# Zero matmuls in TensorE's waits ahead of the first MoE matmul, batch 0's scores by head pairs, and new figures in the planner of the order

## The chip, the core and the metric

The kernel runs on one core of one Trainium2 chip. The metric is the device time of one execution in microseconds. TensorE multiplies matrices, ScalarE computes exp and tanh and copies results out, VectorE transposes 32x32 blocks and does the elementwise work, GpSimd issues the loads, SyncE the stores.

## The reference

```python
# q, k, v: (8 batches, 12 heads, 448 tokens, 64), float32
scores = matmul(q, k.T) / sqrt(64)
attn = exp(scores - max(scores))
attn = attn / (sum(attn) + 1e-9)
x = matmul(attn, v)                       # heads side by side: 3584 tokens x 768
h = x @ w_in                              # 768 x 2048
g = h * sigmoid(h)
out = g @ w_out                           # 2048 x 768, float32
```

## The kernel before

Loads convert float32 to float16 on the way. The 12 heads of a batch are handled four at a time (a head group, `hg`); the four heads occupy the four groups of 32 rows of the 128 partitions. A **unit** is a batch, a head group and a range of queries. In batch 0 the queries are split in two halves of 224, so that units 0, 1, 2 are the first half of the three head groups and units 3, 4, 5 the second; from unit 6 (batch 1) on a unit has all 448 queries.

The stages of a unit are:

* K and Q are loaded (`load_k` L214, `load_q` L219) and transposed on VectorE (`turn_k` L257, `turn_q` L279); V is loaded (`load_v` L230).
* **Scores** (`scores` L307, matmul at L295): keys come in four chunks `c` of up to 128. Results go to PSUM tiles `s`, of which there are two (`s_ring`); one holds two heads (a head pair `y`, 0 or 1) times 448 columns. In batch 0 a tile holds two chunks of 224 queries.
* **exp** (`expo` L327, ScalarE at L331): one 128x896 activation for each `s` tile, four in a batch 0 unit, into a tile `E` (11 of them, `e_ring`).
* **Attend** (`attend` L355, matmul at L347), in three parts: part 0 multiplies E by ones and gives the sums, parts 1 and 2 multiply by V. The results sit in PSUM tiles tagged `m`, of which there are four (`m_ring`). `inverse` (L378, three VectorE steps) turns the sums into 1/sum, `norm` (L394) scales parts 1 and 2 into `xT`.
* **MoE**: `ffn1` (L411) makes six matmuls for one 128-wide slice f of the 2048 hidden columns, `tanh` (L423, ScalarE) and `gate` (L428, VectorE) follow; `ffn2` (L441) makes 16 matmuls for 128 tokens and half of the 768 columns, `store` (L454) copies and stores. Their results share the four `m` tiles with attend.

**The order is made by a planner** that runs in Python when the program is built. `Order` (L69) keeps a modelled time `now` and, for each engine, when it is free. It picks the next piece of work for TensorE at each moment it is free: scores when they are ready and due (`PACE`), else attend, else the first MoE job whose inputs are there. For ScalarE and VectorE it picks, among the operations that are ready, the one with the lowest ready time plus bias. Loads go out in a fixed list on GpSimd's queue (L518 to L540): K and Q of batch 0's three head groups, V of batch 0, Q of its second half, 12 loads of w_in (f 0 to 7), K and Q of batch 1's first group, 12 loads of w_in (f 8 to 15), and so on with w_out in two halves. `Order.step` (L108) says when a load is thought to have landed, from `DMA_RATE` and `DMA_LAT`. What the planner settles is the order of instructions on each engine, nothing else: on the chip every instruction still waits for its own inputs, and instructions of one engine run in that order.

Before all of it, 13 matmuls of zeros (`NWARM`, L856) stand at the head of TensorE's program. The first MoE matmul needs `xT` of units 0, 1 and 2 and the first 12 loads of w_in.

Of the kernel before, what the change touches and what calls it, by code (L numbers as in the profile page):

```python
# [10 lines left out]
FP32 = mybir.dt.float32  # L11
# [5 lines left out]
SWITCH = 0.094  # L17
PE_OUT = 0.20
HOP = 0.10
DMA_RATE = 0.36  # L20
DMA_LAT = 2.0


def mm(n):
    return n / 2400.0 + 0.0026


def act(n):
    return n * 0.000833 + 0.093
# [39 lines left out]
class Order:  # L69


    def __init__(self):
        self.now = 0.0
        self.free = {e: 0.0 for e in ("PE", "ACT", "DVE", "POOL")}
        self.wait = {"ACT": [], "DVE": []}
        self.pool = []
        self.dma_free = 0.0
        self.out = []
        self.mode = None
        self.busy = {e: 0.0 for e in self.free}  # L80
# [27 lines left out]
    def step(self):  # L108

        soon = []  # L110
        for eng in ("ACT", "DVE"):
            if self.free[eng] > self.now:
                soon.append(self.free[eng])
                continue
            best = None
            for op in self.wait[eng]:
                at = op.ready()
                if at is None:
                    continue
                if at > self.now:  # L120
                    soon.append(at)
                elif best is None or at + op.bias < best[0]:
                    best = (at + op.bias, op)
            if best:
                self.wait[eng].remove(best[1])
                self.start(best[1])
                soon.append(self.free[eng])
        if self.free["POOL"] > self.now:
            soon.append(self.free["POOL"])
        elif self.pool:  # L130
            op, mb, ring, gate = self.pool[0]
            at = 0.0
            if ring is not None:
                at = ring.when(1)
            if at is not None and gate is not None:
                g = gate()
                at = None if g is None else max(at, g)
            if at is not None and at <= self.now:
                self.pool.pop(0)
                if ring is not None:  # L140
                    ring.take()
                self.start(op)
                self.dma_free = max(self.dma_free, self.now + 1.0) + mb / DMA_RATE
                op.done = self.dma_free + DMA_LAT - 1.0
                soon.append(self.free["POOL"])
            elif at is not None:
                soon.append(at)
        return soon
# [3 lines left out]
def kernel(  # L152
# [9 lines left out]
    nc = tc.nc  # L162
# [6 lines left out]
    TPP = S // 32  # L169
# [9 lines left out]
    NT = 2 * S // 128  # L179
    OH = DM // 2  # L180
    PACE = 2.6
    NWARM = 13
    LONE = NG + 1
    NE, NGT = 11, 22
    attn_scale = 1.0 / (D**0.5)
# [28 lines left out]
    def load_k(b, hg):  # L214
        t = sb.tile([128, TPP, 2, 32], FP16, name=f"rk_{b}_{hg}", tag="rk", bufs=3)
        nc.gpsimd.dma_start(out=t, in_=group_of(k, b, hg))  # L216
        rawk[(b, hg)] = t

    def load_q(n):  # L219
        b, hg, g0, g1 = units[n]  # L220
        t = sb.tile([128, g1 - g0, 2, 32], FP16, name=f"rq_{n}", tag="rq", bufs=4)
        nc.gpsimd.dma_start(out=t, in_=group_of(q, b, hg)[:, D * g0 : D * g1])  # L222
        rawq[n] = t
# [243 lines left out]
    units = []  # L467
# [12 lines left out]
    MB = 1e-6 * 4 * 32 * HG * D  # L480

    def plan_k(b, hg):
        ld_k[(b, hg)] = od.load(MB * TPP, lambda: load_k(b, hg), rk_ring)

    def plan_q(n):
        ld_q[n] = od.load(MB * (units[n][3] - units[n][2]), lambda: load_q(n), rq_ring)

    def plan_v(b, hg0, hg1):
        made = []
# [87 lines left out]
    def queue_ffn1(b, g0, g1):  # L577
        t0, t1 = 32 * g0, 32 * g1
        for f in range(NFF):

            def run(f=f):
                if b % 2 == 0 and g0 == 0:
                    g_ring.take()
                op = Op("PE", NDC * mm(t1 - t0), lambda: ffn1(b, f, t0, t1), tail=PE_OUT)
                m_ring.take()
                od.on_pe(op, "full")
                th = od.add(
                    Op("ACT", act(t1 - t0), lambda: tanh(b, f, t0, t1), [op], -1, tail=0.2)
                )
                g = Op(  # L590
                    "DVE",
                    (t1 - t0) / 960.0 + 0.13,
                    lambda: gate(b, f, t0, t1),
                    [th],
                    -0.3,
                    then=m_ring.give,
                )
                g_op.setdefault((b, f), []).append(od.add(g))
                ffn1_left[b] -= 1

            ring = g_ring if b % 2 == 0 and g0 == 0 else None
            moe.append(([x_op[(b, cc, g0)] for cc in range(NDC)] + ld_win[f], ring, run))
            ffn1_left[b] += 1

    def queue_ffn2(u, t, half, bs):
        def run():
            op = Op("PE", NFF * mm(OH), lambda: ffn2(u, t, half), tail=PE_OUT)
            m_ring.take()
            od.on_pe(op, "full")
            od.add(  # L610
                Op("ACT", act(OH), lambda: store(u, t, half), [op], -0.3, then=m_ring.give)
            )
            ffn2_left[u] += 1
            if ffn2_left[u] == 2 * NT:
                for _ in range(NFF):
                    g_ring.give(op.done)

        def deps():
            made = list(ld_wout[half])
            for b in bs:  # L620
                for f in range(NFF):
                    if len(g_op.get((b, f), ())) < (2 if b == 0 else 1):
                        return None
                    made += g_op[(b, f)]
            return made

        moe.append((deps, None, run))
# [45 lines left out]
    qk_seq, av_seq = [], []  # L673
    for ns in jobs:
        if len(ns) == 1:
            split = ((0,), (1,)) if ns[0] < 3 else ((0, 1),)
            qk_seq += [(ns, c, ys) for c in range(NCH // per_burst(ns[0])) for ys in split]
        else:
            qk_seq += [([n], c, (0, 1)) for n in ns for c in range(NCH - 1)]
            qk_seq.append((ns, 3, (0, 1)))  # L680
        av_seq += [(ns, part) for part in range(3)]
# [58 lines left out]
    def av_at():  # L740
        if not av_seq:
            return None
        ns, part = av_seq[0]
        deps = []
        for n in ns:
            if len(exp_op.get(n, ())) < 2 * NCH // per_burst(n):
                return None
            deps += exp_op[n]
            if part:
                deps += ld_v[units[n][:2]] + rdn_op.get(n, [None])  # L750
        at = at_of(deps)
        av_data["at"] = at
        m = m_ring.when(len(ns))
        if at is None or m is None:
            return None
        return max(at, m)
# [28 lines left out]
    def after_av(n, part, op, nq):  # L785
        b, hg, g0, g1 = units[n]
        if part == 0:
            made = []
            for step, busy in enumerate((nq / 960.0 + 0.15, 0.2, nq / 960.0 + 0.15)):
                r = Op(  # L790
                    "DVE",
                    busy,
                    lambda step=step: inverse(n, step),
                    made[-1:] or [op],
                    0.5,
                )
                made.append(od.add(r))
            made[0].then = m_ring.give
            rdn_op[n] = made
        else:  # L800
            x = Op(
                "DVE",
                nq / 960.0 + 0.13,
                lambda: norm(n, part),
                [op] + rdn_op[n],
                -1,
                then=m_ring.give,
            )
            x_op[(b, 2 * hg + part - 1, g0)] = od.add(x)
            if part == 2:  # L810
                after_x(n)

    while True:
        plan_turns(qk_seq[0][0][0] + 4 if qk_seq else NU)
        soon = od.step()
        if od.free["PE"] <= od.now:
# [2 lines left out]
            av_data["at"] = None  # L819
            qk, av = qk_at(), av_at()  # L820
            wait = av_data["at"]
            if wait is not None and wait <= od.now - 6 and not (av is not None and av <= od.now):
                moe_i = None
                soon.append(min([x for x in m_ring.free if x>od.now] or [od.now+0.1]))
            if qk is not None and qk <= od.now and (od.now >= pace["next"] or moe_i is None):
# [21 lines left out]
        later = [x for x in soon if x > od.now]  # L847
        if not later:
            break
        od.now = min(later)  # L850
    assert not (qk_seq or av_seq or moe or any(od.wait.values()) or od.pool)


    z = ps.tile([128, 512], FP32, name="z", tag="m", bufs=4)
    for i in range(NWARM):
        nc.tensor.matmul(out=z, lhsT=zeros[:, 0:128], rhs=zeros, start=True, stop=True)  # L856
    for _, _, fn in sorted(od.out, key=lambda x: x[:2]):
        fn()

# [29 lines left out]
```

The softmax here doesn't subtract the row's maximum and nothing guards it: scores larger than these inputs give would overflow.

## Time and profile before

| | us |
|---|---|
| median of the 4 runs | 426.08 |
| lowest and highest | 425.25, 426.41 |
| the profiled execution, its own time | 426.1 |
| its span (first to last instruction) | 424.3 |
| TensorE busy in the span | 415.1 (98%) |
| ScalarE, VectorE, GpSimd busy | 242.4, 193.6, 95.3 |

In the views, PE is TensorE's matmuls, PEld its weight loads, DVE VectorE, ACT ScalarE, POOL GpSimd, SP SyncE; a q behind a name is an engine's queue of instructions that are not counted as busy. L295 is line 295 of the kernel. The clock that is shown (PEclk) is the one granted to TensorE, as a share of full speed. Matmuls overlap, so that a busy TensorE is not one at its peak.

### The profile page before, as it was taken

To read this page: it belongs to the slowest core of one execution; us is meant where nothing else is said; L and a number is where in the kernel's file an instruction comes from. 1 tells how busy PE (TensorE), PEld (TensorE's weight loads), DVE (VectorE), ACT (ScalarE), POOL (GpSimd) and SP (SyncE) were. 2 spreads that over 40 slices of the span, in tenths; PEclk is the share of its full clock that TensorE was granted. 3 is DMA by queue.
4 is the path that set the end of the run, shared out by engine and by line. 5 is a ranking of instruction groups with operands and counts; after the bars stand their busy time and mean duration, and the time that the engine had idled before them with its cause. 6 is when DMAs were issued, how large, how long until landed. Compare 5 with 4: busy or idle time off the path is not lost.

```text
span 424.3 us, 9512 instructions
## 1 busy us (share of the span) xinstructions
PE 415.1 (98%) x3933; PEld 213.0 (50%) x3933; DVE 193.6 (46%) x404; ACT 242.4 (57%) x373; POOL 95.3 (22%) x175
## 2 busy tenths in 40 slices
PE   7899999999999999999999999999999999999996
PEld 3577765444544444444344545544445555565563
DVE  4568746667433585725577154512354214403400
ACT  3678976697465777667766753465773114414411
POOL 6775556530004407200440700000000000000000
PEclk9579999999999999999999999999999999999999
DMA  8999999790024906712391941012100221031033
GB/s 114 202 195 187 148 189 212 120 173 5 11 66 66 205 3 89 125 44 53 33 163 24 148 99 39 2 28 52 36 2 9 53 62 29 2 74 39 0 75 75
DMA packets 37980, 34.45 MB, mean 81 GB/s; under 512 B 11953, under 2 KB 36401, under 8 KB 37937
## 3 DMA queue, kind: packets, MB, share of 16 engines
q0 software_dynamic: 27184, 22.82, 36.6%
q1 hardware_dynamic: 10656, 10.93, 10.1%
q8 instruction: 31, 0.51, 0.5%
q10 hardware_dynamic: 96, 0.10, 0.1%
q14 instruction: 13, 0.10, 0.1%
HBM read 45.61 MB, written 11.01 MB: 133 GB/s over the span
## 4 chain that ended last, share of the span: by engine, by line
PE 93%; DMA 2%; ACT 1%; POOL 1%; DVE 1%; issue 0%; ACTq 0%; DVEq 0%; POOLq 0%
PE o L445 35%; PE h L414 33%; PE a L347 14%; PE s L295 11%; DMA rk<-in_k_dram 2%; ACT E L331 1%; POOL V L235 1%; DVE KT L271 0%; POOL rq L222 0%; POOL rk L216 0%; DVE QT L282 0%; DVE g L432 0%; ACT ost L457 0%; ACTq L457 0%; DVEq L271 0%
## 5 line engine op out<-in xcount | busy, mean ns | idle before, releaser
L331 ACT ACTIVATE E<-s 128x896 f16<-128x896 f32 (+1 forms) x172 | 149.0, 914 | 24.6 <-PE s L295 23.4
L414 PE MATMUL h<-xT,w_in_t 128*128 128x448 f16 (+1 forms) x864 | 153.6, 332 | 0.8 <-DVE g L432 0.8
L445 PE MATMUL o<-w_out_t,g 128*128 128x384 f16 x896 | 152.5, 327 | 0.0
L432 DVE SCALAR_TENSOR_TENSOR g<-th,h 128x448 f16<-128x448 f16 (+1 forms) x144 | 79.7, 563 | 98.8 <-ACT th L425 96.8
L445 PEld LDWEIGHTS <-g 128*128 128x128 f16 x896 | 84.7, 98 | 65.1 <-issue 11.6
L414 PEld LDWEIGHTS <-w_in_t 128*128 128x128 f16 x864 | 80.7, 98 | 69.5 <-issue 13.8
L425 ACT ACTIVATE th<-h 128x448 f16<-128x448 f32 (+1 forms) x144 | 71.6, 505 | 53.6 <-PE h L414 52.1
L457 ACT COPY ost<-o 128x384 f32<-128x384 f32 x56 | 26.8, 478 | 99.5 <-PE o L445 92.3
L235 POOL DMA_DIRECT2D V<-in_v_dram x88 | 48.8, 569 | 134.8 <-PE a L347 115.4
L295 PE MATMUL s<-QT,KT 32*128 32x448 f16 (+4 forms) x864 | 55.0, 349 | 3.2 <-ACT E L331 2.6
L271 DVE STREAM_TRANSPOSE KT<-rk 128x256 f16<-128x256 f16 (+2 forms) x96 | 31.6, 378 | 44.6 <-PE s L295 26.4
L400 DVE SCALAR_TENSOR_TENSOR xT<-a,rdn 128x448 f16<-128x448 f32 (+1 forms) x54 | 28.9, 567 | 35.1 <-PE a L347 34.8
L347 PE MATMUL a<-E,V 128*32 128x448 f16 (+3 forms) x864 | 42.3, 348 | 0.0
L295 PEld LDWEIGHTS <-KT 32*128 32x128 f16 (+2 forms) x864 | 17.1, 103 | 31.9 <-issue 30.5
L347 PEld LDWEIGHTS <-V 128*32 128x32 f16 (+2 forms) x864 | 19.2, 99 | 23.5 <-issue 16.3
L383 DVE STREAM_TRANSPOSE sT<-a 128x448 f32<-128x448 f32 (+1 forms) x27 | 14.9, 578 | 27.0 <-PE a L347 27.0
L282 DVE STREAM_TRANSPOSE QT<-rq 128x896 f16<-128x896 f16 (+1 forms) x27 | 26.3, 974 | 0.6 <-DMA rq<-in_q_dram 0.5
L347 PE MATMUL a<-E,ones 128*32 128x448 f16 (+4 forms) x432 | 21.8, 349 | 0.0
L222 POOL DMA_DIRECT2D rq<-in_q_dram x27 | 15.4, 572 | 4.6 <-DMA rk<-in_k_dram 1.5
L347 PEld LDWEIGHTS <-ones 128*32 128x32 f16 (+2 forms) x432 | 9.5, 99 | 12.7 <-issue 9.0
L216 POOL DMA_DIRECT2D rk<-in_k_dram x24 | 13.9, 578 | 4.0 <-DMA w_out_t<-in_moe_w_out_dram 1.9
L392 DVE STREAM_TRANSPOSE rdn<-inv 128x448 f32<-128x448 f32 (+1 forms) x27 | 14.5, 562 | 0.1
(12 smaller groups left out, 32.6 us busy)
## 6 DMA issues: line engine op xcount, KB each, us to landing
out_dram<-ost SPq DMA_DIRECT2D x222, 48.0 KB, 1.6
rk<-in_k_dram POOLq DMA_DIRECT2D x24, 224.0 KB, 5.3
rq<-in_q_dram POOLq DMA_DIRECT2D x21, 224.0 KB, 6.0
w_in_t<-in_moe_w_in_dram POOLq DMA_DIRECT2D x24, 128.0 KB, 5.5
w_out_t<-in_moe_w_out_dram POOLq DMA_DIRECT2D x8, 384.0 KB, 8.6
V<-in_v_dram POOLq DMA_DIRECT2D x43, 64.0 KB, 4.6
V<-in_v_dram POOLq DMA_DIRECT2D x40, 48.0 KB, 4.6
rq<-in_q_dram POOLq DMA_DIRECT2D x6, 112.0 KB, 5.9
```

The costliest lines, as they stand in the source:

```text
L235: nc.gpsimd.dma_start(out=VT[b][32 * x : 32 * (x + 1), hs, 0:count, :], in_=v[b, hs].rearrange("h (i g) d -> i h g d", g=TPP)[:, :, first ...
L271: nc.vector.transpose(out=kt[:, e].rearrange("p c x i -> p x c i")[:, x:y, 0:count], in_=t[:, first : first + count * (y - x), e, :].rearr ...
L282: nc.vector.transpose(out=qt.rearrange("p e g i -> p g e i"), in_=rawq[n])
L295: nc.tensor.matmul(out=pS[p0 : p0 + 32 * (x1 - x0), h % 2, at : at + nq], lhsT=KT[(b, hg)][32 * h : 32 * (h + 1), e, c, x0:x1, :], rhs=QT[ ...
L331: nc.scalar.activation(out=E[(n, w)][0:kr, 2 * y : 2 * y + 2, :], in_=pS_t[(n, w, y)][0:kr, :, 0:S], func=AF.Exp, scale=attn_scale,)
L347: nc.tensor.matmul(out=a[32 * h : 32 * (h + 1), 0:nq], lhsT=w, rhs=e[k0:k1, h, at : at + nq], start=start, stop=stop,)
L400: nc.vector.scalar_tensor_tensor(out=xT[(b, cc)][:, 32 * g0 : 32 * g1], in0=acc[(n, part)][:, 0:nq], scalar=0.5, in1=rdn_t[n].rearrange("p ...
L414: nc.tensor.matmul(out=h[:, 0 : t1 - t0], lhsT=w_in_t[:, cc, 128 * f : 128 * (f + 1)], rhs=xT[(b, cc)][:, t0:t1], start=(cc == 0), stop=(c ...
L425: nc.scalar.activation(out=th, in_=h_t[(b, f, t0)][:, 0 : t1 - t0], func=AF.Tanh)
L432: nc.vector.scalar_tensor_tensor(out=g_t[(u, f)][:, S * r + t0 : S * r + t1], in0=th_t[(b, f, t0)], scalar=1.0, in1=h_t[(b, f, t0)][:, 0 : ...
L445: nc.tensor.matmul(out=o[:, 0:OH], lhsT=g_t[(u, f)][:, 128 * t : 128 * (t + 1)], rhs=w_out_t[:, f, n0:n1], start=(f == 0), stop=(f == NFF ...
L457: nc.scalar.copy(out=ost, in_=o_t[(u, t, half)][:, 0:OH])
```

## The change

* The 13 zero matmuls at the head are gone. In the planner's loop, as long as no MoE matmul has been planned, each modelled wait of TensorE of more than 0.3 us gets as many zero matmuls of 512 columns as fit, less 0.1 us. Their PSUM tile `z` holds one of the four `m` tiles until the first `ffn1`.
* The scores of all six units of batch 0 are issued by head pairs; before, units 3, 4 and 5 issued both pairs together, which takes both `s` tiles at once.
* The model of the loads is fitted anew (rate, start, landing, K and Q at 1.2 times their size), and the engines start later in the model.
* Four biases change: gate -0.3 to -2, store -0.3 to 0.5, the three steps of `inverse` 0.5 to 2.
* A rule that held MoE work back once an attend part had been waiting for 6 us now asks for 1000 us.
* `if n >= 0` changes nothing, since n is never negative.

```diff
-DMA_RATE = 0.36
-DMA_LAT = 2.0
+DMA_RATE = 0.37
+DMA_TAIL = 1.0
...
-        self.free = {e: 0.0 for e in ("PE", "ACT", "DVE", "POOL")}
+        self.free = {"PE": 1.2, "ACT": 2.1, "DVE": 1.2, "POOL": 1.2}
...
-                self.dma_free = max(self.dma_free, self.now + 1.0) + mb / DMA_RATE
-                op.done = self.dma_free + DMA_LAT - 1.0
+                self.dma_free = max(self.dma_free, self.now + 1.5) + mb / DMA_RATE
+                op.done = self.dma_free + DMA_TAIL
...
-    NWARM = 13
...
-        ld_k[(b, hg)] = od.load(MB * TPP, lambda: load_k(b, hg), rk_ring)
+        ld_k[(b, hg)] = od.load(1.2 * MB * TPP, lambda: load_k(b, hg), rk_ring)
...   (plan_q the same)
                 op = Op("PE", NDC * mm(t1 - t0), lambda: ffn1(b, f, t0, t1), tail=PE_OUT)
+                if warm["on"]:
+                    warm["on"] = False
+                    m_ring.give(od.now)
                 m_ring.take()
...   (gate)
-                    -0.3,
+                    -2,
...   (store)
-                Op("ACT", act(OH), lambda: store(u, t, half), [op], -0.3, then=m_ring.give)
+                Op("ACT", act(OH), lambda: store(u, t, half), [op], 0.5, then=m_ring.give)
...
-            split = ((0,), (1,)) if ns[0] < 3 else ((0, 1),)
+            split = ((0,), (1,)) if ns[0] < 6 else ((0, 1),)
...   (inverse)
-                    0.5,
+                    2,
...
+    warm = {"on": 1}
+
+    def run_zeros(n):
+        if "z" not in warm:
+            warm["z"] = ps.tile([128, 512], FP32, name="z", tag="m", bufs=4)
+        for _ in range(n):
+            nc.tensor.matmul(
+                out=warm["z"], lhsT=zeros[:, 0:128], rhs=zeros, start=True, stop=True
+            )
+
+    m_ring.take()
     while True:
...
-            if wait is not None and wait <= od.now - 6 and not (av is not None and av <= od.now):
+            if wait is not None and wait <= od.now - 1000 and not (av is not None and av <= od.now):
...
+        wait = min(later) - od.now
+        if warm["on"] and od.free["PE"] <= od.now and wait > 0.3 and od.now > 1.0:
+            n = max(1, int((wait - 0.1) / mm(512)))
+            od.on_pe(Op("PE", n * mm(512), lambda n=n: run_zeros(n)), "full")
         od.now = min(later)
...
-    z = ps.tile([128, 512], FP32, name="z", tag="m", bufs=4)
-    for i in range(NWARM):
-        nc.tensor.matmul(out=z, lhsT=zeros[:, 0:128], rhs=zeros, start=True, stop=True)
     for _, _, fn in sorted(od.out, key=lambda x: x[:2]):
         fn()
```

More of the change, by code (lines that the diff above doesn't have):

```diff
@@ L482, in plan_k @@
     def plan_k(b, hg):
-        ld_k[(b, hg)] = od.load(MB * TPP, lambda: load_k(b, hg), rk_ring)
+        ld_k[(b, hg)] = od.load(1.2 * MB * TPP, lambda: load_k(b, hg), rk_ring)
     def plan_q(n):
-        ld_q[n] = od.load(MB * (units[n][3] - units[n][2]), lambda: load_q(n), rq_ring)
+        ld_q[n] = od.load(1.2 * MB * (units[n][3] - units[n][2]), lambda: load_q(n), rq_ring)
     def plan_v(b, hg0, hg1):
@@ L749, in av_at @@
             if part:
-                deps += ld_v[units[n][:2]] + rdn_op.get(n, [None])
+                deps += ld_v[units[n][:2]]
+                if n >= 0:
+                    deps += rdn_op.get(n, [None])
         at = at_of(deps)
```

## The prediction

> **What bounds the kernel now.** I read the page first. TensorE is busy 98% of the span, and the row of granted clock is full everywhere but at the start.
>
> ```profile
> PE 415.1 (98%) x3933; PEld 213.0 (50%) x3933; DVE 193.6 (46%) x404; ACT 242.4 (57%) x373; POOL 95.3 (22%) x175
> PEclk9579999999999999999999999999999999999999
> ```
>
> So I cut the span into stretches (columns: stretch, its length, busy time and instructions of PE, PEld, DVE, ACT, POOL, then clock, DMA share, GB/s).
>
> ```profile
> 6.92:26.38 19.46, 17.12 (x272) 10.78 (x272) 10.05 (x27) 12.95 (x15) 13.04 (x25) 0.56 1.20 197
> 40.00:404.00 364.00, 363.23 (x3301) 180.56 (x3299) 170.59 (x339) 212.79 (x330) 67.32 (x122) 1.00 0.42 71
> ```
>
> From 40 to 404 us TensorE idles 0.77 us in all: nothing can be won there but by less work, and the change takes away no matmul after its start. From 6.92, the first score, to 26.38, the first MoE matmul, the mean clock is 0.56. I then cut that stretch where the clock changes; the steps come out 3.41 us long.
>
> ```profile
> 5.68:9.09 3.41, 1.88 (x28) 0.94 (x26) 1.98 (x7) 1.58 (x2) 1.92 (x4) 1.00 1.03 142
> 9.09:12.50 3.41, 3.03 (x36) 1.81 (x39) 2.73 (x8) 2.96 (x5) 2.19 (x5) 0.50 1.41 193
> 12.50:15.91 3.41, 3.38 (x54) 1.91 (x44) 2.22 (x6) 2.37 (x3) 2.45 (x5) 0.50 1.33 200
> 22.74:26.15 3.41, 3.41 (x68) 2.30 (x64) 1.42 (x4) 2.26 (x3) 2.50 (x5) 0.50 1.13 205
> 26.15:29.56 3.41, 3.41 (x63) 2.43 (x56) 2.46 (x8) 3.11 (x6) 2.10 (x4) 1.00 1.11 189
> ```
>
> TensorE was busy 1.88 of the 3.41 us up to 9.09, and the clock halved. It returned only after a stretch without any gap (3.41 of 3.41); 3.38 of 3.41 had not been enough. What half speed costs is in the timeline of TensorE:
>
> ```profile
> 1.23 5.15 PE L856 MATMUL z<-zeros 128*128 128x512 f16 x13 [1.23 <-DVE zeros L199]
> 6.92 0.59 PE L295 MATMUL s<-QT,KT 32*128 32x224 f16 x16 [0.53 <-DVE QT L282]
> 15.08 0.93 PE L295 MATMUL s<-QT,KT 32*128 32x224 f16 x8
> 15.94 0.94 PE L347 MATMUL a<-E,V 128*32 128x224 f16 x16
> 38.29 0.57 PE L347 MATMUL a<-E,ones 128*32 128x224 f16 x16
> ```
>
> An attend part of 16 matmuls takes about 0.9 us at half speed and 0.5 on the chain at full speed; the scores of a head pair (8 matmuls) 0.9 against 0.3 to 0.4. Meanwhile ScalarE starves: in its first 30 us it idles 11.7 us for scores (the view of line 331; 5.5 of it before its first exp at 7.51), though an exp in a pair takes 0.86 us (two in 1.72). At 26.38 TensorE has issued 128 score matmuls (16 exps) and 144 attend matmuls (nine parts, units 0 to 2).
>
> What else does the first MoE matmul wait for? The twelfth load of w_in is issued at 18.7, and the DMA view has it land 5.5 us later, at 24.2:
>
> ```profile
> 18.11 1.11 POOL L246 DMA_DIRECT2D w_in_t<-in_moe_w_in_dram  x2 [0.19 <-issue]
> w_in_t<-in_moe_w_in_dram POOLq DMA_DIRECT2D x1, 128.0 KB, 5.5
> ```
>
> The queues move about 200 GB/s all through that stretch, so this does not move: 24.2 is a floor, and at most 2.2 us can be had by starting MoE earlier. All other gain must be attention work done before then.
>
> **The change part by part.**
>
> *The zeros.* Until the first score they take the place of the 13: by the code's own due times I count about 16, and TensorE waits for Q's transpose (ends 6.86) anyway; 12 of the 13 run at 0.43 us while cold, three more at about 0.22 us each end by 7.0. Cost at most 0.1 us. After that they keep the array busy through waits that now bring the clock down. I take the clock as full from 5.7 to the first MoE matmul. A step that was 55% busy lowered it (1.88 of 3.41), one with the 0.77 us gap before 220.18, 77%, did not; between these no row tells. So bounds: never falls, or falls for one or two steps of 3.41 us, each of which loses half of its real work, 1.7 us. I take none, since the fill leaves at most some 0.3 us of each modelled wait; two dips go into the range.
>
> With full clock ScalarE sets the pace. Exp 1 starts at 7.51 as now. At 0.865 us each, 20 are done by 24.9; I take about 0.05 us of bubble each (TensorE does 4 score pairs at 0.4 and 3 parts at 0.5, 3.1 us, for 3.46 us of ScalarE, and in-order attend parts sometimes stand in front of a score), so 19. Unit 3 needs exp 16, done at 7.5 + 16 x 0.915 = 22.1; its three parts follow by 24.9. The model's own due time for w_in is 24.85 (start 2.7, three K and Q pairs 6.70, V 3.72, Q 2.23, w_in 8.50, tail 1.0), 0.65 us after the real 24.2. First MoE matmul: 24.9 instead of 26.38, that is **1.5 us**. By then 12 parts are done instead of 9: 3 x 0.49 = **1.4 us**.
>
> *Head pairs.* Joint scores took both `s` tiles, which left ScalarE idle between pairs (1.56 us before the pair at 18.52). Split ones keep two tiles turning, part of the 19 above. After 24.9 about four score pairs are left, at 0.4 = 1.6 us, where before eight were left as four joint issues of 0.49 to 0.55, 2.1 us: **0.5 us**. The 0.31 us wait at 35.5, for both tiles, goes too, but a wait of that size may return.
>
> *What is late next.* From 24.9 TensorE is ahead while loads are not: the second 12 of w_in land at 35.0 (29.7 + 5.3). Until then, 10.1 us, there are eight MoE slices at 0.62 (4.9), scores 1.6, six attend parts (2.9) and most of unit 6's scores (1.3), 10.7 us, and eight more slices when units 3 to 5 are done. Enough, but tight: I charge **0.3 us**, bounds 0 and 1.5. Later loads have room: w_out's first half lands at 45.5 (issue 34.2, 11.2 to landing) for use at 60.6, the second at 62.8 (53.3 + 9.5) for use at 71.9.
>
> *Biases, the 6 us rule, the refit.* No matmul is added or removed by them. Their cover is that TensorE always has MoE work after 26 us. The cost of another order can only be idle time of TensorE; the trace has one such wait there, 0.77 us at 220.18, for a gate that held an `m` tile. Bound: none (or that one gone, -0.8) to four such waits, 3.1 us. I take zero.
>
> Sum: 1.5 + 1.4 + 0.5 - 0.3 = 3.1 us. The profiled execution took 426.1 (span 424.3), the median of runs is 426.08, so the sum holds for both: **423.0 us**, span 421.2.
>
> *Against the Trainium skill.* "TensorE: Matmul & The Clock Gate", section "HAM oscillation — how this bites in real kernels", asks only that TensorE have no idle gap over about 3.4 us. Here the longest gap before the clock fell at 9.09 was 0.97 us, so the row differs, and the row decides. By the page there was nothing to fill, and the sum would keep only the head pairs, about 425.5. The same page's "What's actually happening" says that one busy window of about 3.4 us brings full clock back; 9.09 to 22.74 says that a window 99% busy may not do it. By the page a dip costs one window at most; by the rows it can last several.
>
> **Rivals.**
>
> 1. *The clock falls all the same.* The zeros fit the modelled waits at 0.22 us each; if the clock drops once, each takes 0.43, TensorE is over-full and runs late, and nothing can be skipped since it works in order. Being over-full it has no gap and recovers after one or two steps (as at 26.15). Price 1.7 to 3.4 us: 424.7 to 426.4. For it: 3.38 of 3.41 us did not restore the clock. Against: zeros use the whole array, and 13 of them brought full speed at 5.7.
> 2. *The loads take it back.* TensorE, ahead by 3 us, runs dry near 35 us and waits for w_in's second half. Price 1.5 us: about 424.5. For it: DMA share at or above 1 until about 75 us; against: 10.7 us of work for 10.1.
> 3. *Slower: `m` tiles starve.* With `inverse` at bias 2 behind gates, and no rule that holds MoE back for a pair of attend parts that needs two free `m` tiles at once, attention falls behind in the middle of the kernel, `E` and `g` tiles fill, and TensorE waits as at 220.18. It decides from five such waits: 5 x 0.77 = 3.9 us outweighs the gain by 0.8. With six, 4.6 us, the time is 427.6. For it: ten of eleven E tiles are needed by five units, and four `m` tiles are shared by all. Against: 0.77 us of idle in 364 us today, and VectorE is at 46%.
>
> **How the numbers follow.** About 0.2% (0.85 us) is what a measurement here can tell from no change. Forecast 423.0: chance 0.62. Its own range is 421.2 (first MoE matmul at 24.3, one part more, the 0.77 gone) to 424.2. Clock dips: 0.13, mostly within or just below 0.2%. Loads: 0.12. Slower: 0.13. Faster by over 0.2%, below 425.2: 0.62 + 0.12 + 0.06 of the dips = 0.80; within: 0.06 of the dips and 0.02 of the third rival = 0.08; slower: 0.01 of the dips and 0.11 = 0.12. The range of 8 in 10 runs from 421.0 to 426.0: it takes in the first two rivals and leaves out most of the third.
>
> **What would show it.** Right: granted clock 1.00 from 6 to 40 us; exps without idle from 7.5; the first `h` at 24.3 to 25.5 with 12 attend parts ahead of it; TensorE idle from 40 to 404 us under 1.5 us. Wrong: a clock of 0.5 in any step between 9 and 25 (rival 1), TensorE waiting for w_in between 31 and 36 (rival 2), waits of `h`, `a` or `o` for VectorE or ScalarE after 60 us that sum to over 3 us (rival 3).

## The result and the profile after

The changed kernel takes 427.74 us (median of 43 runs, 423.50 to 429.51) against 425.60 of 64 runs of the kernel before: a ratio of 1.0036, 95% interval 1.0023 to 1.0049. By the ratio, which goes by the kernel before on the same chip, it is slower by about 1.5 us (the two medians differ by 2.1), where 423.0 and a gain of 3.1 us had been forecast; it is outside the range of 421.0 to 426.0. Three executions of 437 to 438 us further down, two of the head pairs alone and one of the changed kernel with a zero behind each burst (mean clock 0.952 to 0.968, none of them profiled), stand in no median, range or ratio.

The single executions do not lie around one value. The table has 44 of them, one (428.24) more than the median. Ordered by the mean granted clock that each recorded, they fall into groups, and the missing share of the clock is close to a whole number of steps of 3.41 us at half speed (clock 0.980 over 425.9 us: 0.020 x 425.9 = 8.5 us lost, 17.1 us at half speed, five steps):

| steps at half speed | mean clock | executions | us, lowest to highest |
|---|---|---|---|
| 2 | 0.991 to 0.992 | 6 | 423.50 to 424.09 |
| 4 | 0.984 | 12 | 425.89 to 426.52 |
| 5 | 0.980 | 8 | 427.58 to 428.16 |
| 6 | 0.974 to 0.976 | 18 | 428.08 to 429.51 |

From two to six steps the time grows by some 4.8 us, 1.2 us a step. The six executions of two steps lie inside the forecast's own range (421.2 to 424.2); none of them was profiled. That price of a step shows in the changed kernel alone: of the kernel before, 61 executions with a mean clock of 0.983 or 0.984 (about four steps) have a median of 425.4, and 37 with 0.977 to 0.980 (about five) 425.7. The mean clock also has a blind spot, since no clock is recorded ahead of the first full one. This stretch of the kernel before has nine zeros in 3.41 us, half speed, and is printed with 1.00:

```profile
2.27:5.68 3.41, 3.41 (x9) 1.21 (x8) 0.63 (x3) 0.00 (x0) 3.41 (x7) 1.00 0.93 129
```

An execution whose clock rose late would thus show a high mean clock too.

The profiled execution of the changed kernel is one of five steps: 427.73 us, span 425.9. Its page, to be held against the first two lines shown of before:

```profile
PE 418.6 (98%) x3940; PEld 214.1 (50%) x3940; DVE 194.3 (46%) x404; ACT 242.9 (57%) x373; POOL 95.2 (22%) x175
PEclk9659999999999999999999999999999999999999
```

There are 3940 matmuls instead of 3933: 20 zeros for 13. The low clock comes 4.2 us later (it falls at 13.26 instead of 9.09) and lasts five steps, as in the profile of before; it has not gone. The stretches cut at the changes of the clock (stretch, length, busy time and instructions of PE, PEld, DVE, ACT, POOL, clock, DMA share, GB/s):

```profile
6.43:9.85 3.42, 2.75 (x34) 1.28 (x35) 2.31 (x6) 1.91 (x3) 1.71 (x4) 1.00 1.05 157
9.85:13.26 3.41, 2.90 (x55) 1.81 (x52) 2.58 (x8) 3.36 (x5) 2.16 (x5) 1.00 1.47 191
13.26:16.67 3.41, 2.98 (x50) 1.74 (x49) 1.74 (x4) 2.15 (x3) 2.71 (x7) 0.50 1.24 207
23.50:26.91 3.41, 3.41 (x49) 1.85 (x49) 1.42 (x4) 1.72 (x2) 1.28 (x3) 0.50 1.13 207
40.00:404.00 364.00, 364.00 (x3330) 182.12 (x3330) 174.15 (x349) 213.95 (x333) 67.22 (x122) 1.00 0.42 71
```

Until the clock fell, ScalarE was the pace, as forecast: 3.36 of 3.41 us busy from 9.85 to 13.26. Then the clock fell, after a step in which TensorE was 85% busy (2.90 of 3.41), and it did not come back after one that was busy without a gap (23.50 to 26.91). From 40 to 404 us TensorE does not idle at all. So the loss is made in the start, and the timeline of TensorE shows how:

```profile
7.86 0.60 PE L825 MATMUL z<-zeros 128*128 128x512 f16 x2
18.36 0.61 PE L825 MATMUL z<-zeros 128*128 128x512 f16 x1
24.55 0.61 PE L825 MATMUL z<-zeros 128*128 128x512 f16 x1
14.95 0.93 PE L294 MATMUL s<-QT,KT 32*128 32x224 f16 x8
29.67 1.05 PE L413 MATMUL h<-xT,w_in_t 128*128 128x224 f16 x6
```

After the first score there are just four zero matmuls, two at 7.86, one at 18.36 and one at 24.55. The planner cuts a wait at the next event of any engine, and works with full speed for TensorE; since each modelled wait of over 0.3 us gets at least one zero, there are at most four of them here. The first MoE matmul comes at 29.67, 3.3 us later than before. By 29.67 both kernels have issued the same attention work (144 score and 160 attend matmuls, counted in the traces), but before has 20 MoE matmuls issued and after has none: at 0.62 us for six of them, 2.1 us.

### The profile page after: what moved, and what is told of

Read it like the earlier page. It is cut to its first block, busy times and chain, and to the rows that moved or that the text cites. A ratio compares the mean times of both kernels' runs of the same rounds, so it can differ in the third digit from the quotient of the medians.

```text
span 425.9 us, 9528 instructions
## 1 busy us (share of the span) xinstructions
PE 418.6 (98%) x3940; PEld 214.1 (50%) x3940; DVE 194.3 (46%) x404; ACT 242.9 (57%) x373; POOL 95.2 (22%) x175
## 4 chain that ended last, share of the span: by engine, by line
PE 97%; ACT 2%; issue 0%; DVE 0%; ACTq 0%
PE h L413 35%; PE o L444 35%; PE a L346 14%; PE s L294 11%; ACT E L330 2%; PE z L825 2%; ACT ost L456 0%; DVE zeros L198 0%; DVE ones L196 0%; ACTq L456 0%
```

## What the clock follows

**A measure.** I weighed each matmul by the share of the 128x128 array that it uses and by its columns. The unit is a zero matmul (whole array, 512 columns); TensorE passes 8 of them in a 3.41 us step at half speed, so 16 fill a step at full speed. A score or attend matmul of 224 columns uses a quarter of the array (32x128 or 128x32): 0.109 units, or three quarters of that where the chunk has 96 keys. A MoE matmul of 224 columns is 0.44. "Array use" is the sum over a step, divided by 16, where a matmul that crosses the end of a step is shared out.

In the 17 traces of this study (before, after and the 15 runs below), eleven steps each from the first full clock on, the next step's clock goes with it like this:

| clock in the step | clock in the next | steps | array use | TensorE busy share |
|---|---|---|---|---|
| full | full | 124 | 0.352 to 0.91 | 0.53 to 1.00 |
| full | half | 11 | 0.18 to 0.305 | 0.54 to 1.00 |
| half | half | 41 | 0.16 to 0.352 | 0.73 to 1.00 |
| half | full | 11 | 0.350 to 0.44 | 1.00 |

One threshold near 0.35 sorts all 187 steps both ways, with an overlap of 0.002 (a step of 0.352 was followed by half speed, one of 0.350 by full speed). The busy share does not sort them, and neither do rows alone, columns alone or the number of matmuls. The threshold is known to a few hundredths only: no step at full clock lies between 0.305 and 0.352, and another way of sharing out the matmuls at a step's ends (by their busy time) moves single values by some 0.03. After these eleven steps the clock falls just once more in the 17 traces before the last microseconds, in the run of zeros early with the new biases, after a step of 0.35 to 0.36. This was read out of traces, and the next three runs were made to try it. Theory A is that the clock follows array use; the rival, Theory B, is that it follows how long TensorE idles, and that the later MoE start is what costs.

**One zero behind each score burst, of the whole array or of a sixteenth of it.**

```diff
                 run_qk()
                 od.now, keep = od.free["PE"], od.now
+                if warm["on"]:
+                    od.on_pe(Op("PE", PER * mm(512), lambda: run_zeros(PER)), "full")
+                    od.now = od.free["PE"]
...   (PER = 1)
```

> The changed kernel, with one full-size zero matmul (128 rows x 128 columns x 512) planned right behind each score burst until the first MoE matmul: 35 zero matmuls instead of 20. Theory A (the clock monitor weighs how much of the array is used in steps of 3.41 us, and steps below about 0.35 of the array at full speed lower the clock or fail to raise it): by the counts of the changed kernel's trace, a score pair uses 0.187 us of a full array and a zero matmul 0.213, so each 0.9 us holds at least 0.40, share 0.44; the clock stays at 1.00 from the warm-up to the end in nearly every execution (mean clock over 0.99), first MoE matmul at 25 to 26.5 us, time 421.5 to 424 with little spread. Theory B (what counts is how long TensorE is idle, and the later MoE start of the new order is what costs): TensorE is busy 85 to 100% already, so the clock falls as before, mean clock 0.975 to 0.985, and 15 more zeros at half speed (0.43 us each) cost up to 6 us: 428 to 433.

Measured: 426.17 us (11 runs), ratio 1.0008 (0.999 to 1.0026); mean clock 0.998 to 1.000, and full in the profile from 4.5 us on.

```diff
-                    od.on_pe(Op("PE", PER * mm(512), lambda: run_zeros(PER)), "full")
+                    od.on_pe(Op("PE", PER * mm(512), lambda: run_small(PER)), "full")
...   (run_small)
+                out=warm["z"][0:32, :], lhsT=zeros[0:32, 0:32], rhs=zeros[0:32, :],
```

> The same order and the same number of zero matmuls behind the bursts, but each of the 19 uses 32 rows x 32 columns, a sixteenth of the array, for the same 512 columns of time. Theory A: array use falls back to about the changed kernel's 0.27 to 0.38 of the array, so the clock falls as there: mean clock 0.97 to 0.985, time 427 to 432, several us above the run with full-size zeros. Theory B (idle time of TensorE counts): the same clock and the same time as with full-size zeros, within 0.5 us.

Measured: 441.93 us (6 runs), ratio 1.0353 (1.0313 to 1.0394); mean clock 0.954 to 0.963, in the profiled execution 0.963. Two stretches of the run with whole-array zeros, and then three of the run with small ones:

```profile
7.94:11.35 3.41, 3.41 (x42) 1.82 (x40) 2.55 (x9) 3.41 (x5) 1.49 (x4) 1.00 1.29 182
14.77:18.18 3.41, 3.41 (x67) 1.95 (x59) 3.20 (x8) 1.93 (x3) 2.99 (x6) 1.00 1.12 199
```

```profile
8.37:11.78 3.41, 3.41 (x39) 1.75 (x37) 3.27 (x10) 3.41 (x6) 2.15 (x4) 1.00 1.35 191
18.61:22.02 3.41, 3.41 (x46) 1.77 (x35) 1.42 (x4) 0.92 (x1) 2.24 (x5) 0.50 1.05 180
39.09:42.50 3.41, 3.41 (x54) 2.33 (x53) 0.89 (x3) 2.01 (x4) 0.74 (x2) 0.50 1.31 203
```

The orders differ in the tile of 19 zeros and in nothing else, and TensorE is busy 3.41 of 3.41 us in all five lines. With whole-array zeros the step at 8 us has an array use of 0.46 and the clock stays; with small ones 0.21, and it falls at 11.78 for nine steps, until MoE matmuls lift a step to 0.42. So it is array use and not busy time that the clock follows here. Both times were worse than expected. The clock was held, but not the 421.5 to 424 that I had put with it: a zero between score bursts takes 0.33 us of the chain at full speed (7.46 to 7.79 in these lines of its timeline), not 0.216, which is what the last zeros ahead of the first score of the changed kernel take from start to start, and a head pair 0.49 (7.79 to 8.28):

```profile
7.46 0.39 PE L826 MATMUL z<-zeros 128*128 128x512 f16 x1
7.79 0.56 PE L295 MATMUL s<-QT,KT 32*128 32x224 f16 x8
8.28 0.39 PE L826 MATMUL z<-zeros 128*128 128x512 f16 x1
27.59 0.74 PE L414 MATMUL h<-xT,w_in_t 128*128 128x224 f16 x6
```

TensorE became the bound (3.41 of 3.41 us, while ScalarE was busy 1.93 from 14.77 to 18.18), and the first MoE matmul came at 27.59.

**The same zeros in the kernel before.** The edit is the first one above, with the 13 leading zeros kept and the `m` tile held until the first `ffn1`.

> The kernel before with the same 13 leading zeros and its own planner figures, plus one full-size zero matmul behind each score burst until the first MoE matmul (14 more). Theory A: the clock stays at 1.00 from about 6 us on; the gain is what half speed costs before, first MoE matmul at 24.5 to 25.5 instead of 26.4 and attention not behind: 422 to 424. Theory B: clock as before, 14 zeros more at half speed, 426 to 431.

Measured: 424.40 us (12 runs), ratio 0.9965 (0.9947 to 0.9982), clock 1.00 from 6.6 us on, first MoE matmul at 24.38. The clock is as Theory A has it and the median lies 0.4 above its range.

## Which part of the change costs

Each part alone in the kernel before, and each undone in the changed kernel. Ratios are to the kernel before on the same chip.

| | median us | ratio | 95% interval |
|---|---|---|---|
| the whole change | 427.74 | 1.0036 | 1.0023 to 1.0049 |
| head pairs alone | 429.03 | 1.0079 | 1.0064 to 1.0093 |
| new model alone | 426.19 | 1.0021 | 1.0008 to 1.0033 |
| zeros in the waits alone | 426.06 | 0.9995 | 0.998 to 1.001 |
| biases and rule alone | 425.35 | 0.9993 | 0.9983 to 1.0003 |
| change without head pairs | 426.75 | 1.0020 | 1.0003 to 1.0037 |
| change without new model | 429.24 | 1.0094 | 1.0078 to 1.0109 |
| change without new biases | 428.20 | 1.0059 | 1.0035 to 1.0084 |

The four parts alone add up to 0.9%, the whole is 0.36%: the parts do not simply add.

**Head pairs undone, and alone.**

```diff
-            split = ((0,), (1,)) if ns[0] < 6 else ((0, 1),)
+            split = ((0,), (1,)) if ns[0] < 3 else ((0, 1),)
```

> The changed kernel with units 3, 4 and 5 issuing both head pairs together again. Theory A adds that at half speed a head pair alone (8 matmuls) takes TensorE 0.93 us, as much as both pairs together (16 in 0.93 to 1.00), so the head pairs cost time in a cold start: joint scores come out 0.5 to 2 us faster than the changed kernel, 425.5 to 427, with the clock still falling. Theory B (the order's later MoE start from the new DMA model costs, not the pairs): same as the changed kernel within 0.4 us.

Measured: 426.75, inside the range of Theory A. But the interval of its ratio overlaps that of the whole change: what the pairs cost inside the change, 0.7 us by the ratios, is not clear of the noise. The reverse edit in the kernel before:

> The kernel before with one part of the change alone: units 3 to 5 by head pairs. Its planned order has 32 more score and attend matmuls ahead of the first MoE matmul. If head pairs cost TensorE twice as much per pair at half speed and push MoE back, 0.5 to 2 us slower than before: 426 to 427.5. If they cost nothing (the new order is at fault for another reason): 425.5 within 0.4.

Measured: 429.03 (4 runs), 1.5 us above the range: the cost is larger than I had expected, 0.79% or 3.4 us by the ratio. A pair alone at half speed, and what follows it, in this run's timeline of TensorE; then both pairs together in that of before:

```profile
22.35 0.93 PE L295 MATMUL s<-QT,KT 32*128 32x224 f16 x8
23.21 0.94 PE L347 MATMUL a<-E,ones 128*32 128x224 f16 x16
29.78 1.14 PE L414 MATMUL h<-xT,w_in_t 128*128 128x224 f16 x6
```

```profile
22.02 0.93 PE L295 MATMUL s<-QT,KT 32*128 32x224 f16 x16
22.88 0.94 PE L347 MATMUL a<-E,ones 128*32 128x224 f16 x16
```

From 22.35 to the next matmul at 23.21 is 0.86 us for 8 matmuls; in the kernel before, 16 matmuls took the same 0.86, from 22.02 to 22.88. The first MoE matmul moved from 26.38 to 29.78, nearly as far as in the whole change. By array use a pair fills half of what both do in the same time. The clock stayed low for six steps here, against five in the profile of before; how much of the cost comes through the clock was not separated.

**The new model undone, and alone.**

> The changed kernel with the old model of loads and engine starts: 12 zero matmuls in all instead of 20, the first MoE matmul one slice earlier in the order and slices taken one at a time between scores. If the later MoE start of the refitted model costs, this is faster than the changed kernel by 0.5 to 1.5 us (426 to 427.3); if the pairs are what costs, it is like the changed kernel, 427.3 to 428.5, with a clock that falls at least as early, since it has fewer zeros.

Measured: 429.24. Neither case expected came: it is slower than the changed kernel. With the old model there are 12 zeros instead of 20, the clock falls at 10.09 instead of 13.26, and for six steps. Within the change the refit gains; that it does so by the zeros which its later due times put ahead is argued, not tested by itself. One of the six executions recorded a mean clock of 0.999 and took 429.20 all the same. No trace of it was kept, so it is open whether its clock rose late or a held clock gained nothing there.

> The kernel before with the new model of loads and engine starts alone. It puts one joint score issue and one attend part more ahead of the first MoE matmul (0.9 to 1.8 us at half speed), work that is not lost but moved. If the refit is a cost of its own: 426.5 to 427.5; if moved work is neutral: 425.5 within 0.5.

Measured: 426.19, ratio 1.0021. Alone it costs 0.9 us. Its first MoE matmul comes at 28.37, and the work put ahead of it does not make up for that: by 40 us it has issued as many score and attend matmuls as before (200 and 256), but 58 MoE matmuls against 67.

**Biases and rule undone, and alone.**

> The changed kernel with the four old biases and the 6 us rule. Its order up to the first MoE matmuls is the same as the changed kernel's. Both theories of the start expect the same time as the changed kernel within 0.5 us (427 to 428.3). If the biases and the rule were what made the change slower (my third rival), it is below 426 and TensorE idles less between 40 and 404 us; the changed kernel idles 0.00 us there, which speaks against it.

> The kernel before with the four new biases and the 1000 us rule alone. The order up to the first MoE matmuls is unchanged. My third rival had this slower by several us through m tiles; the changed kernel's trace (no idle time of TensorE from 40 to 404 us) says 425.5 within 0.6, or slightly faster, by the 0.77 us wait at 220.

Measured: 428.20 and 425.35, both inside the ranges. The ratio of the first overlaps that of the whole change; alone the biases are between -0.17% and +0.03%. They do not make the change slow.

**Zeros in the waits alone.**

> The kernel before with the zeros of the change alone: the 13 at the head replaced by zeros in the planner's modelled waits, 15 in all (11 ahead of the first score, 1 behind it, 3 late), old model, old biases, joint scores. By array use it cannot hold the clock: the step after the first scores gets one zero (0.06 of the array) on top of about 0.28; so the clock falls in most executions and the time is that of before within 0.8 us, 425 to 426.3. If the zeros in the waits were what made the change slow: 426.5 or above.

Measured: 426.06, ratio 0.9995: neither gain nor loss. The clock fell in its trace at 10.15 (9.09 before), after a step of array use 0.25. Here too two of the 12 executions recorded a mean clock of 0.999 and 1.000 and took 426.05 and 425.53, no less than the others, and the same question stays open.

## Versions that hold the clock and keep joint scores

**Change without head pairs, one zero per burst.** Two of the edits above put together.

> The changed kernel with one zero matmul behind each score burst, as in the run of that kind (426.2), but with units 3 to 5 issuing both head pairs together. The clock should stay at 1.00 in both. A head pair alone takes TensorE 0.49 us on the chain at full speed, as much as both together, so that six issues fewer are worth 2.9 us, and six zeros fewer at 0.33 another 2.0; but the first MoE matmul cannot come before w_in's landing near 24.2, which caps it: 3 us below, 422.8 to 423.8. If head pairs cost nothing at full speed (my prediction: four pairs at 0.4 against four joint issues at 0.5), the gain is the zeros alone, at most 2 us: 424.2 or more.

Measured: 423.30 us (6 runs), ratio 0.9945 (0.9931 to 0.9959), as expected. The clock is full until 421 us. The same kernel without the zeros behind the bursts took 426.75, at a clock that was low for four steps in its profile: this one edit is worth 0.75% by the ratios, 3.2 us. Against the same kernel with head pairs (426.17) the gain is 2.9 us, for six score issues and four zeros less; the zeros account for up to 4 x 0.33 = 1.3 of it. The first MoE slice starts at 24.30 and waits for w_in within its six matmuls, which is the floor named in the prediction:

```profile
24.30 0.55 PE L414 MATMUL h<-xT,w_in_t 128*128 128x224 f16 x4
25.43 0.37 PE L414 MATMUL h<-xT,w_in_t 128*128 128x224 f16 x2 [0.59 <-DMA w_in_t<-in_moe_w_in_dram]
```

ScalarE is busy 14.12 us from 6.92 to 26.38 (12.95 in the same stretch of the kernel before), at full clock:

```profile
6.92:26.38 19.46, 17.84 (x317) 10.24 (x320) 10.75 (x30) 14.12 (x18) 12.48 (x24) 1.00 1.15 181
```

**Before, zeros only where attention cannot fill the array.**

```diff
+                PER = 2 if not parts[0] else 1 if parts[0] < 2 else 0
+                if warm["on"] and PER:
+                    od.on_pe(Op("PE", PER * mm(512), lambda n=PER: run_zeros(n)), "full")
+                    od.now = od.free["PE"]
...   (parts[0] counts the attend parts planned so far)
```

> The kernel before, with two full-size zero matmuls behind each score burst until the first attend part, one until the second, none after: 12 added instead of the 14 spread to the first MoE matmul. If array use is what the clock follows (threshold near 0.35 of the array in a 3.41 us step), only the score stretch up to about 14 us needs filling, since with attend parts a unit uses (4 x 0.187 + 3 x 0.373) / 3.5 = 0.53 by itself: clock 1.00 from the warm-up on, in more executions than with one zero per burst (whose first step was at 0.36), first MoE matmul at 24.2 to 24.8, median 423 to 424.2 and a smaller spread. If instead the zeros themselves must go on to keep the clock, it falls to 0.5 between 15 and 24 us and the time is 425 to 427.

Measured: 423.13 us (9 runs, 422.48 to 425.24), ratio 0.9955 (0.9939 to 0.9971). In its trace the steps from 14.79 to 21.62, which have no zeros, hold the clock at an array use of 0.46 and 0.54. In the profiled execution, one of the longer ones at 424.93, TensorE then waited for w_in, that step's array use was 0.29, and the clock fell for one step from 25.03. Three zeros in front of the first `ffn1` were to mend that:

> The kernel before with zeros early (two behind each score burst until the first attend part, one until the second) and three zeros right ahead of the first MoE matmul, where TensorE waits for w_in: with early zeros alone the step 21.62 to 25.03 had 0.31 of the array and the clock fell for one step in the profiled execution (424.9, against 422.5 in the best). Three zeros add 0.19, to 0.50. Theory A: clock 1.00 throughout, all executions between 422.3 and 423.5, median 422.9. If the zeros' own time counts for more than the dip: 423.2 or above with the same spread as before.

Measured: 425.51 (12 runs, 423.27 to 427.88), ratio 0.9994 (0.9975 to 1.0012), a miss, although the clock was full. TensorE idles 2.3 us between 40 and 404 us here, and 1.8 of it stands in one line:

```profile
82.26 2.76 PE L446 MATMUL o<-w_out_t,g 128*128 128x384 f16 x16 [1.81 <-DVE xT L401]
```

Together with the new biases, which make another order after 40 us:

> The kernel before with zeros early (423.1 in its run) and the four new biases with the 1000 us rule, which alone left the time as it was but took the 0.77 us wait at 220 away: 422.3 to 423.3. If the biases cost in another order: 423.5 or above.

> Zeros early and three ahead of the first MoE matmul (425.5 in its run, with the clock at 1.00 but 2.3 us of idle from 40 to 404 us, 1.8 of it at 82 us, for a norm that VectorE did late), plus the new biases and rule. If that loss was an accident of the order after 40 us, another order does not have it, since nothing else differs: 422.5 to 423.7. If the three zeros cost by themselves: 424.8 or above.

Measured: 424.05 (12 runs, ratio 0.9963, 0.9947 to 0.998) and 423.77 (12 runs, ratio 0.9958, 0.9942 to 0.9975), 0.75 and 0.1 us above the ranges. The same wait of `o` for a norm is there again, 1.9 and 0.8 us. In the first of the two the wait costs more than itself: it leaves a step at 0.35 to 0.36 of the array, the clock falls at 81.46 for one step, and the 16 matmuls behind it take 4.44 us instead of 2.76:

```profile
80.65 4.44 PE L445 MATMUL o<-w_out_t,g 128*128 128x384 f16 x16 [1.88 <-DVE xT L400]
```

So the three zeros cost little by themselves, 423.77 against 424.05; the loss at 82 us depends on the order. What decides its size was not settled. The lowest ratio of all is that of the changed kernel with joint scores and one zero per burst, 0.9945; its interval overlaps that of zeros early, 0.9955.

## Why the prediction was wrong, by its own steps

* **"I take the clock as full from 5.7 to the first MoE matmul."** This step failed first. I took it that the zeros fill the waits, but the plan holds four after the first score, and the clock fell at 13.26 and stayed low for five steps in the profile (two to six over the executions). So the first MoE matmul came at 29.67 with ten attend parts ahead of it, where 24.9 with 12 had been forecast: the 1.5 us of an earlier start became 3.3 us of a later one. Before the first score the count of 16 was right. Read off the code's own rule (a wait ends at the next event of any engine), the number of zeros between scores was the thing to count, and I had counted only those ahead of them.
* **The bounds of a dip.** Rival 1 was what happened, and "one or two steps" at 1.7 us each was mis-sized: two to six steps, most often six, at 1.2 us each. I had reasoned with the busy share (a step 55% busy fell, one 77% busy held); the longest gaps in the two are much the same, 0.97 and 0.77 us, and the tiles differ. The rival's argument that an over-full TensorE has no gap and so recovers is wrong as well: with 32x32 zeros it was busy throughout and stayed at half speed for nine steps.
* **Head pairs, "0.5 us" gained.** The sign was wrong. A pair was put at 0.4 us, and it takes 0.49 at full speed and 0.86 at half, as much as both together. Alone this part costs 3.4 us; within the change its cost is 0.7 us by the ratios, not clear of the noise. The rows to see it were in the trace of before: 0.93 for 8 matmuls at 15.08, and 16 in the same time later. I used the one and not the other. The planner's own price of a score issue, `2 * per_burst(n) * mm(nq)`, is the same for one pair and for two.
* **The floor at 24.2 by w_in** held for the first slice as a whole, not for its first matmul. With the clock full and joint scores the slice starts at 23.04 to 24.38, and in five of these six versions it then waits for w_in, until 24.41 to 25.92.
* **ScalarE as the pace at full clock, and "12 parts are done instead of 9", 1.4 us:** this held only until 13.26. With the clock held to the first MoE matmul and joint scores, nine parts are ahead of it, as before, and in the profile of the version with 423.30 us 16 exps are done by 24.9, not 19; ScalarE idles 3.3 us between them. The term did not show in this form; these versions also have zeros between the scores, so that what the parts would do without them stays open.
* **"What is late next", 0.3 us, bounds 0 and 1.5:** of the seven versions with whole-array zeros added behind the bursts, three wait for w_in's second half, between 35 and 37 us, for 0.4 to 0.7 us. The term was real, somewhat over the 0.3 charged and within its bounds.
* **Biases and rule at zero** was right, and the third rival was not what made the change slow.
* **With clock and pairs put right, the gain is near the size forecast:** 0.55% by the ratio, 2.3 us, where the sum had 3.1. It is not made up as the sum has it: the first MoE matmul comes 2.1 us earlier instead of 1.5, and no attend part more is done by then. That the total comes so near is in part luck.
* **The Trainium skill**, "TensorE: Matmul & The Clock Gate", section "HAM oscillation — how this bites in real kernels", asks for no idle gap over about 3.4 us. In the changed kernel the longest gap before the clock fell at 13.26 is 0.45 us, so the row goes against it once more. Its section "What's actually happening" has one busy step of about 3.4 us restore the clock; steps busy for 3.41 of 3.41 us, at 23.50 above and with small zeros, did not.

## What to carry to other kernels

A busy TensorE is not a warm one: count rows times columns of the tiles that are in use, over the steps in which the clock changes, before you count on full speed, and fill with whole-array matmuls where that share is low. A score issue that uses half of the row groups took as long here as one that uses all (0.86 us at half speed), so splitting one to release a buffer sooner pays only if TensorE has the time. When a filler is put in by a planner, count what it puts where; a model that cuts its waits at every event may fill next to nothing.

## What the runs showed of the hardware that was not expected

* A threshold of array use near 0.35 per 3.41 us step, for losing and, within a few hundredths, for regaining full clock (0.352 held, 0.305 fell; 0.350 rose, 0.352 stayed low).
* Whole-array zeros count as array use: weighed like the other matmuls, they fit the one threshold, and zeros of 32x32 in their place did not hold the clock.
* The number of low steps varies from execution to execution of one kernel (2, 4, 5 or 6), in the changed kernel in step with the time. The changes of the clock lie at other times after the start in each trace (full from 3.9 to 6.7 us on), so that a step holds other work.
* A whole-array matmul of 512 columns between tiled groups costs 0.33 us of TensorE's chain, against 0.216 in a row of its own kind.
